# A fused S4 convolution and gated MLP on one core: the order of all operations written as one explicit list

## The chip, the cores and the metric

The kernel runs on one core of a Trainium2 chip. A core has four compute engines, TensorE (PE), VectorE (DVE), ScalarE (ACT) and GpSimd (POOL), and a fifth, SyncE (SP), which issues transfers; each takes its instructions strictly in the order in which the program gives them to it, and waits at the head of its queue until what an instruction needs is there. The metric is device time in microseconds (us), the median over several runs. The profile's span is the time from the first to the last recorded event of one execution; the device time is a little longer.

## The reference

With x = u of shape (1, 2048, 640), the output is a gated sum of two branches:

```python
g = sigmoid((x * gate_w).sum(-1, keepdims=True))
return g * a + (1 - g) * b
```

Branch a is a state space (S4) layer. For each of the 640 channels it forms a kernel K of length 2048 from 128 complex modes, and convolves u with it by FFTs of length 4096:

```python
P = exp(logdA[:, :, None] * l[None, None, :])      # logdA = dt * A, l = 0..2047
K = einsum('dn,dnl,dn->dl', Cc, P, dB).real
y = irfft(rfft(pad(u)) * rfft(pad(K)))[:L] + u * Dskip
```

Branch b is a gated MLP with a product over positions:

```python
z = gelu(x @ w_in)                     # (2048, 1728)
z1, z2 = z[..., :864], layernorm(z[..., 864:])
b = (z1 * (w_sp @ z2 + b_sp)) @ w_out  # w_sp is (2048, 2048)
```

## The kernel before

**How the work is cut.** The 2048 positions are 16 tiles of 128 rows or 8 blocks of 256. The 640 channels are split in two: h0 (480 channels) and h1 (160). The stages, with the names that the profile shows:

- `z2_tile` (L592, 16 tiles): x by the second half of w_in into the two-bank accumulator `two`, then on ACT a gelu (L596) and a tanh for the gate (L598), and sums for the layer norm on ACT or DVE. `z1_tile` (L624, four x groups of four tiles each): the first half of w_in, gelu on ACT into `zt` (L415), stored to DRAM.
- `sp_block` (eight blocks tb 0 to 7): `w_sp` by z2n (L812, 16 matmuls of 128x256 for each of seven tiles of 128 features, recorded in chunks of four), the sum with b_sp on DVE (L816), the product with z1 on DVE (L818), w_out (L832), and a scaling by 1 - g into `ob` (L836 on DVE or ACT). `ob` goes to DRAM except for the last rows, which stay in `acc`.
- `k_exps`, `k_tables`, `eights`: for eight groups of 80 channels, c 0 to 7, tables of exponentials and sines, on ACT, DVE and POOL. POOL or DVE makes the arguments (`si`, `ci`, through L361), ACT takes the sine (L415); ACT loads a table of its own for each of gelu, exp and sine when it changes over.
- `k_sub` (L1045, L1046, eight in all: six for h0, two for h1): 320 small matmuls that make K from the tables. `k_store` and `k_expand` put K out to DRAM and back in the layout of a transform.
- `s1_u` (L651) and `conv_s1` (L1134): the first stage of the transform, of u (from the tile `xf`) and of K, each stored to DRAM (`FU_d`, `FK_d`).
- `conv_s2` (32 steps k for h0, 16 for h1): second stage of u (mu, L1181, copied to `us` on ACT), second stage of K (mk, L1188, `ps_s2k`), their product `p` on DVE (L1190), the first stage back (mv, L1196), copied to `vs` on ACT (L1198).
- `conv_vt` (L1204): 16 DVE transposes of `vs`, three groups of four for h0 (g 0 to 2) and one for h1 (g 3). `conv_i2` (L1276, L1278): the last stage back, which needs all transposes of its half; `i2_out` adds g times it to the MLP's rows (DVE L1212, or ACT L1229 and an add at L1231 on DVE or POOL). A few matmuls without use (L1282) stand ahead of the first of them. Then the output goes out.

**What sets the order.** Nothing in this code runs when it is called. `Plan.add` records each operation as a task: the engine or engines that may do it with a cost for each, the function that emits it, what it reads and writes, and which buffers of a ring it holds. 1810 tasks are recorded. `Plan.run` then goes through them when the program is built and emits them in the order that it finds, and that order is what each engine's queue has. Before the change, `run` is a list scheduler: it keeps a clock for each engine, and when one is free gives it the ready task with the longest remaining path (`bl`) plus a bias. The biases come from the calls and from a table, `TUNE`, keyed by function, line within the function and index. Where a task has several engines, the one that is free takes it. A cost of 1.3 us is charged where ACT's function set changes, and a task may have a `lag` on another: `k_sub` asks for 4.0 us behind the one before it.

Buffers that bear on the order: two of `two` (two PSUM banks each), two of `g` and two of `x` in PSUM; in SBUF, two of `wT` (the blocks of w_sp) and `z1t`, four of `vT`, two of `ob` and `s1u`, one of `xf`, three of `us`, `fu`, `fk` and `p12`.

Of the kernel before, what the change touches and what calls it, by code (L numbers as in the profile page):

```python
# [25 lines left out]
class Handle:  # L26
# [11 lines left out]
TUNE = {  # L38
    ('conv_s1', 18, None): -5520,
    ('conv_s1', 15, ('g', 0)): -124,  # L40
    ('conv_s1', 19, None): 5553,
    ('conv_s2', 35, None): -5280,
    ('conv_s2', 34, ('h', 0)): 2234,
    ('conv_s2', 34, None): 886,
    ('conv_s2', 10, None): 5448,
    ('conv_s2', 14, None): 3353,
    ('conv_s2', 42, None): 2803,
    ('eights', 6, None): 173,
    ('eights', 13, None): 13956,
    ('i2_out', 15, None): 12,  # L50
    ('k_expand', 28, ('h', 0)): 4849,
    ('k_expand', 28, None): 1375,
    ('k_store', 14, ('h', 1)): 2102,
    ('k_store', 6, ('h', 0)): 8481,
    ('k_sub', 13, ('h', 0)): 2159,
    ('k_tables', 31, ('c', 6)): -12493,
    ('k_tables', 31, None): 8580,
    ('k_tables', 32, ('c', 4)): -777,
    ('k_tables', 32, None): 371,
    ('k_tables', 41, None): 1904,  # L60
    ('k_tables', 30, ('c', 7)): 3564,
    ('k_tables', 29, ('c', 3)): -10091,
    ('k_tables', 29, None): 3002,
    ('k_tables', 6, None): 7128,
    ('k_tables', 18, ('c', 7)): 6367,
    ('k_tables', 17, ('c', 4)): 2780,
    ('k_tables', 17, None): -1891,
    ('k_tables', 36, None): 3593,
    ('k_tables', 20, None): -429,
    ('k_tables', 21, ('c', 2)): -5305,  # L70
    ('k_tables', 21, ('c', 6)): -5859,
    ('k_tables', 38, ('c', 6)): 4382,
    ('k_tables', 38, None): -6392,
    ('main', 151, ('g', 0)): -1177,
    ('main', 151, ('g', 3)): 41101,
    ('main', 155, None): -414,
    ('main', 148, None): -2063,
    ('main', 147, None): -1758,
    ('main', 417, None): -6232,
    ('main', 369, None): 2196,  # L80
    ('main', 437, None): 310,
    ('main', 442, None): -153,
    ('main', 419, None): -10,
    ('main', 421, None): -41,
    ('s1_u', 13, ('h', 1)): -11176,
    ('s1_u', 13, ('n0', 0)): -23393,
    ('s1_u', 13, ('n0', 8)): -7946,
    ('s1_u', 13, None): 3018,
    ('s1_u', 16, ('n0', 10)): -8951,
    ('s1_u', 3, ('n0', 0)): -14093,  # L90
    ('s1_u', 3, ('n0', 10)): 63,
    ('s1_u', 3, None): 84,
    ('s1_u', 18, ('h', 1)): 582,
    ('s1_u', 18, ('n0', 12)): -9089,
    ('s1_u', 14, ('h', 1)): -3707,
    ('s1_u', 14, ('n0', 0)): 7218,
    ('sp_block', 23, ('tb', 6)): 5972,
    ('sp_block', 23, None): -1436,
    ('sp_block', 25, ('tb', 5)): -2260,
    ('sp_block', 20, ('tb', 2)): 14630,  # L100
    ('sp_block', 41, ('tb', 1)): 8742,
    ('sp_block', 41, None): 2551,
    ('sp_block', 47, None): -8196,
    ('sp_block', 3, ('tb', 5)): 4372,
    ('sp_block', 3, ('tb', 7)): -14321,
    ('sp_block', 3, None): -4356,
    ('sp_block', 8, ('tb', 5)): 1880,
    ('sp_block', 6, ('tb', 5)): 321,
    ('tg_build', 22, None): 5697,
    ('tg_build', 6, None): -428,  # L110
    ('tg_build', 20, None): 8012,
    ('tg_build', 9, ('c', 0)): 5213,
    ('tg_build', 9, ('c', 1)): 3260,
    ('x_group', 3, None): -2923,
    ('z1_tile', 17, None): 3575,
    ('z1_tile', 10, ('g', 0)): 774,
    ('z1_tile', 10, ('g', 2)): 1445,
    ('z2_tile', 12, None): 5932,
    ('z2_tile', 19, None): 12871,
    ('z2_tile', 18, ('h', 0)): 6796,  # L120
}
HELPERS = ("dma", "actf", "evac", "<lambda>", "ptt", "pts", "ftt", "fts", "pstt", "S_", "E", "K_", "M_")


class Plan:

    ENG = ("PE", "DVE", "ACT", "POOL", "SP", "NONE")
    SYNC = 0.04  # L130
    OV = {"DVE": 0.08, "ACT": 0.09}
    LAT = {"PE": 0.17, "POOL": 0.8}
# [10 lines left out]
    def add(self, eng, cost, fn, r=(), w=(), hold_=(), fset=None, nbytes=0, hold=0.0, bias=0.0, deps=(), lag=()):  # L143
        f = sys._getframe(1)
        while f.f_code.co_name in HELPERS:
            f = f.f_back
        nm = f.f_code.co_name if len(f.f_code.co_name) < 26 else "main"
        rel = f.f_lineno - f.f_code.co_firstlineno
        ix = next(((v, f.f_locals[v]) for v in ("tb", "c", "g", "h", "n0") if isinstance(f.f_locals.get(v), int)), None)
        bias += TUNE.get((nm, rel, None), 0) + (TUNE.get((nm, rel, ix), 0) if ix else 0)  # L150
# [26 lines left out]
    def run(self):  # L177
        T = self.tasks
        N = len(T)
        succ = [[] for _ in T]  # L180
        for t in T:
            for d in t["deps"]:
                succ[d].append(t["i"])
        bl = [0.0] * N
        for t in reversed(T):
            i = t["i"]
            c = min(t["costs"]) + (2.2 + t["nb"] / 1e6 if t["nb"] else 0.0)
            bl[i] = c + max([bl[s] for s in succ[i]], default=0.0)
        users = {}
        seq, cnt = {}, {}  # L190
        for t in T:
            for h in t["hs"]:
                if h not in users:
                    seq[h] = cnt.get(h.ring, 0)
                    cnt[h.ring] = seq[h] + 1
                users.setdefault(h, [0, 0.0])[0] += 1
        nd = [len(t["deps"]) for t in T]
        rdy = [0.0] * N
        allocs = {k: 0 for k in self.rings}
        freed = {k: [] for k in self.rings}  # L200
        slot = {}
        ready = {e: [] for e in self.ENG}
        free = {e: 0.0 for e in self.ENG}
        dma = 0.0
        cold = 0.0
        fset = None
        done = [False] * N
        order = []
        for t in T:
            if nd[t["i"]] == 0:  # L210
                for e in t["engs"]:
                    ready[e].append(t["i"])
        ev = [0.0]
        while len(order) < N:
            if not ev:
                held = {h.ring: [] for h in slot}
                for t in T:
                    if not done[t["i"]] and any(h in slot for h in t["hs"]) and nd[t["i"]] == 0:
                        print("HELD", t["i"], t["engs"], t["fn"].__qualname__[-20:], t["fn"].__code__.co_firstlineno, [(h.ring, h in slot) for h in t["hs"]])
                raise AssertionError("stuck")  # L220
            now = heapq.heappop(ev)
            while ev and ev[0] <= now + 1e-9:
                heapq.heappop(ev)
            again = True
            while again:
                again = False
                for e in self.ENG:
                    if free[e] > now + 1e-9 and e != "NONE":
                        continue
                    best, bk = None, None  # L230
                    for i in ready[e]:
                        if done[i] or rdy[i] > now + 1e-9:
                            continue
                        t = T[i]
                        ok = True
                        for h in t["hs"]:
                            if h in slot:
                                continue
                            a = allocs[h.ring]
                            n = self.rings[h.ring]  # L240
                            if h.ring not in self.free_order and seq[h] != a:
                                ok = False
                            if a >= n:
                                f = freed[h.ring]
                                if a - n >= len(f) or f[a - n] is None or f[a - n] > now + 1e-9:
                                    ok = False
                        if not ok:
                            continue
                        key = bl[i] + t["bias"]
                        if e == "ACT" and t["fset"] and t["fset"] != fset:  # L250
                            key -= 25.0
                        if bk is None or key > bk:
                            best, bk = i, key
                    if best is None:
                        continue
                    again = True
                    t = T[best]
                    i = best
                    done[i] = True
                    for x in t["engs"]:  # L260
                        ready[x] = [j for j in ready[x] if j != i]
                    c = t["costs"][t["engs"].index(e)]
# [3 lines left out]
                    for h in t["hs"]:  # L266
                        if h in slot:
                            continue
# [1106 lines left out]
```

## Time and profile before

| | us |
|---|---|
| device time, median of 3 runs | 357.02 |
| the runs | 356.61, 357.02, 362.8 |
| span of the profiled execution | 353.6 |
| PE busy (L812 alone) | 309.6 (106.8) |
| DVE busy (L1190 alone) | 286.4 (48.4) |
| ACT busy | 241.8 |
| POOL busy | 153.6 |
| first `k_sub` starts | 105.0 |
| first mk of `conv_s2` h0 starts | 263.0 |
| last p of h0 ends | 303.2 |
| first matmul of `conv_i2` starts | 318.8 |

An engine's busy time is a sum over stages which have different limits, so it says little by itself. The page has a table of the span in 40 slices (each 8.8 us), where each digit is an engine's busy share in tenths, and the trace answers the same for any stretch. The list of waits has, for an engine and a line, what it last waited for: total us, times, longest. The chain is followed back from the last instruction, at each step to what released it. The letters PEld stand for TensorE's weight loads, which run beside its matmuls. PEclk is the clock that TensorE was granted, in shares of full speed.

The table by stages, in words: up to 105 us z2, z1, the first blocks and the first tables; from 105 to 248 the six k_subs of h0 and two of h1 among sp_blocks and `s1_u`, with PE busy for 0.88 to 0.97 of the time; 248 to 264 the last blocks; from 264 `conv_s2` of h0; from 305 to 319 its transposes; then `conv_i2` of h0 mixed with `conv_s2` of h1; from 338 the rest of h1, and the output.

### The profile page before, as it was taken

Reading aid. Unit: us, or ns where it says so; the run is one execution under the profiler, and the core shown is the slowest. Engines: PE = TensorE matmul, PEld = TensorE weight load, DVE = VectorE, ACT = ScalarE, POOL = GpSimd, SP = SyncE. Lnnn points to the kernel's source line nnn. Section 1 sums busy time; section 2 is a strip of 40 time slices with the busy share of each in tenths; the row PEclk is TensorE's granted clock in tenths of the full one; section 3 lists DMA queues with packets and bytes.
Section 4 is the critical chain, followed back from the end, with each engine's and each line's share of the span. In section 5 each row is a group of like instructions: output and inputs, shape, how many; then the busy total and the mean of one; then the engine's idle time right before and its main releaser. Section 6 shows DMA issues by size and latency. Waiting matters only on the chain.

```text
span 353.6 us, 8393 instructions
## 1 busy us (share of the span) xinstructions
PE 309.6 (88%) x3231; PEld 216.9 (61%) x3237; DVE 286.4 (81%) x548; ACT 241.8 (68%) x437; POOL 153.6 (43%) x155
## 2 busy tenths in 40 slices
PE   3899899989899999999699998699999999809982
PEld 3455445857778687878577776477774444405751
DVE  4079996789897949998489758777789999996985
ACT  1658975999784676889876684564538888804842
POOL 3005544600095826773187989434459400203221
PEclk9999999999999999999899999899999999977998
DMA  7988999669981578496592249998958886273404
GB/s 200 205 141 230 199 188 213 193 154 191 249 135 49 135 173 164 114 223 104 152 250 82 61 63 174 197 264 267 230 161 250 222 238 195 61 211 138 141 28 130
DMA packets 110809, 59.89 MB, mean 169 GB/s; under 512 B 78322, under 2 KB 107354, under 8 KB 110770
## 3 DMA queue, kind: packets, MB, share of 16 engines
q1 hardware_dynamic: 108530, 55.33, 63.9%
q0 software_dynamic: 2240, 4.04, 5.4%
q8 instruction: 25, 0.41, 0.5%
q14 instruction: 14, 0.11, 0.1%
HBM read 25.25 MB, written 19.47 MB: 126 GB/s over the span
## 4 chain that ended last, share of the span: by engine, by line
PE 44%; DVE 24%; ACT 10%; issue 7%; DMA 6%; POOL 5%; SPq 2%; ACTq 0%; DVEq 0%; POOLq 0%
PE ps_g L812 13%; DVE p L1190 5%; DVE vs L1204 5%; PE ps_z L592 5%; PE ps_o L832 4%; PE ps_z L624 4%; DMA xf<-in_A_u_dram 4%; PE ps_s2k L1188 3%; POOL ci L361 3%; PE ps_k L1045 3%; PE ps_v L1196 3%; PE ps_k L1046 3%; PE ps_s1k L1134 2%; ACT z2n L596 2%; ACT ET L415 2%
## 5 line engine op out<-in xcount | busy, mean ns | idle before, releaser
L812 PE MATMUL ps_g<-wT,z2n 128*128 128x256 bf16 (+1 forms) x896 | 106.8, 276 | 5.8 <-issue 2.8
L812 PEld LDWEIGHTS <-z2n 128*128 128x128 bf16 (+1 forms) x896 | 90.2, 103 | 22.7 <-issue 8.7
L1190 DVE TENSOR_TENSOR p<-ps_s2k,us 128x960 bf16<-128x960 f32 (+1 forms) x48 | 48.4, 1040 | 1.9 <-PE ps_s2k L1188 0.6
L361 POOL TENSOR_SCALAR ci<-ai 128x640 int32<-128x640 int32 (+1 forms) x8 | 21.5, 2693 | 55.3 <-DVE ai L968 33.2
L361 POOL TENSOR_SCALAR si<-th 128x80 int32<-128x80 f32 x40 | 32.1, 802 | 12.7 <-DVE t3p L761 4.6
L832 PE MATMUL ps_o<-Wout,vT 128*128 128x320 bf16 (+1 forms) x224 | 34.3, 299 | 3.0 <-ACT ob L836 3.0
L624 PE MATMUL ps_z<-xg,Win 128*128 128x512 bf16 (+1 forms) x134 | 31.6, 380 | 0.8 <-ACT zt L415 0.5
L592 PE MATMUL ps_z<-Win,xT 128*128 128x432 bf16 (+1 forms) x160 | 30.4, 346 | 2.1 <-ACT gl L598 2.1
L415 ACT ACTIVATE ET<-ci 128x640 bf16<-128x640 int16 (+1 forms) x40 | 26.0, 677 | 6.9 <-POOL ci L361 3.5
L832 PEld LDWEIGHTS <-vT 128*128 128x128 bf16 (+1 forms) x224 | 21.8, 98 | 13.5 <-issue 4.1
L1045 PE MATMUL ps_k<-ET 128*32 128x33 bf16 x640 | 27.7, 259 | 1.6 <-DVE ET L1028 1.1
L1045 PEld LDWEIGHTS <-ET 128*32 128x32 bf16 x640 | 26.9, 193 | 3.6 <-DVE ET L1028 3.1
L1198 ACT CAST vs<-ps_v 128x480 bf16<-128x480 f32 (+1 forms) x48 | 24.3, 521 | 5.1 <-PE ps_v L1196 4.1
L1046 PE MATMUL ps_k<-ET 128*32 128x33 bf16 x640 | 27.6, 258 | 0.0
L1046 PEld LDWEIGHTS <-ET 128*32 128x32 bf16 x640 | 27.1, 195 | 0.3 <-issue 0.3
L816 DVE TENSOR_TENSOR vT<-ps_g,br 128x512 bf16<-128x512 f32 (+1 forms) x32 | 18.7, 615 | 9.8 <-PE ps_g L812 9.8
L1188 PE MATMUL ps_s2k<-fk,T 128*128 128x480 bf16 (+1 forms) x128 | 25.0, 304 | 1.5 <-DVE p L1190 1.4
L1196 PE MATMUL ps_v<-p,G 128*128 128x480 bf16 (+1 forms) x128 | 25.1, 304 | 0.5 <-DVE p L1190 0.2
L592 PEld LDWEIGHTS <-xT 128*128 128x128 bf16 x160 | 15.5, 98 | 16.3 <-issue 3.0
L415 ACT ACTIVATE mr<-lre 128x320 bf16<-128x320 f32 x66 | 25.1, 457 | 0.0
L422 ACT CAST us<-ps_u 128x480 bf16<-128x480 f32 (+1 forms) x48 | 24.0, 521 | 0.7 <-ACT vs L1198 0.4
L415 ACT ACTIVATE ET<-ai 128x640 bf16<-128x640 int16 (+1 forms) x24 | 15.2, 645 | 12.1 <-DVE ai L968 12.1
(195 smaller groups left out, 618.7 us busy)
## 6 DMA issues: line engine op xcount, KB each, us to landing
FU_d<-s1u SPq DMA_DIRECT2D x16, 240.0 KB, 3.4
fu<-FU_d SPq DMA_DIRECT2D x16, 240.0 KB, 3.9
fk<-FK_d SPq DMA_DIRECT2D x16, 240.0 KB, 3.5
z_d<-zt SPq DMA_DIRECT2D x24, 128.0 KB, 2.5
z1t<-z_d SPq DMA_DIRECT2D x8, 384.0 KB, 4.3
xf<-in_A_u_dram SPq DMA_DIRECT2D x8, 320.0 KB, 3.4
Win<-in_B_w_in_dram SPq DMA_DIRECT2D x2, 1080.0 KB, 6.2
ob_d<-ob SPq DMA_DIRECT2D x12, 160.0 KB, 3.3
```

Of the source, the lines that this page charges most:

```text
L361: eng.tensor_scalar(out=out_, in0=in_, scalar1=s1, scalar2=None, op0=op0)
L415: return add("ACT", cost, lambda e: act.activation(out=out_(), in_=in_(), func=func, scale=scale), r=r, w=w, fset=fs, bias=bias, deps=deps ...
L592: pe.matmul(ps()[:, h, 0:432 + h], lhsT=xT[:, i, 128 * st:128 * st + 128], rhs=Win2[:, i, 432 * h:432 * h + 432 + h], start=(i == 0), stop ...
L624: pe.matmul(ps()[0:fs, ft - f0, :], lhsT=Win1[:, i, 128 * ft:128 * ft + fs], rhs=xg()[:, i, :], start=(i == 0), stop=(i == ND - 1))
L812: pe.matmul(ps()[0:fs, ft - f0, :], lhsT=z2n[:, st, 128 * ft:128 * ft + fs], rhs=wT()[:, st, :], start=(st == 0), stop=(st == NS - 1))
L832: pe.matmul(ps()[:], lhsT=vT[ft // 2]()[0:fs, ft % 2, 128 * r:128 * r + 128], rhs=Wout[0:fs, ft, HD * h:HD * h + HD], start=(ft == 0), sto ...
L1045: pe.matmul(o_, lhsT=ET[:, 0:32, d], rhs=M2[:, :, d], start=True, stop=False, tile_position=(0, 32 * q))
L1046: pe.matmul(o_, lhsT=ET[:, NA:NA + 32, d], rhs=E2[:, :, d], start=False, stop=True, tile_position=(0, 32 * q))
L1188: pe.matmul(ps()[:, i, W * n:W * n + W], lhsT=TK(k + n, i), rhs=fk()[:, j + n, :], start=True, stop=True)
L1190: add("DVE", dv1(2 * NW), lambda e, p12=p12, ps=ps, us=us: vec.tensor_tensor(out=p12()[:, :, 0:NW], in0=ps()[:, :, 0:NW], in1=us()[:, 0:NW ...
L1196: pe.matmul(pv()[:, W * n:W * n + W], lhsT=GV(k + n, i), rhs=p12()[:, i, W * n:W * n + W], start=(i == 0), stop=(i == 1))
L1198: add("ACT", 0.15 + NW / 1170, lambda e, k=k, pv=pv: act.copy(out=X["vs"][h][:, k:k + NK, :], in_=pv()[:, 0:NW].rearrange("p (k d) -> p k ...
```

## The change

`run` no longer schedules. A text, `ORDER`, has three characters for each of the 1810 tasks: two for its number, one for its engine (0 PE, 1 DVE, 2 ACT, 3 POOL, 4 SP). `run` reads it, asserts that every task is there once, that its engine is one of those allowed and that its dependencies come first, takes buffers and emits. `TUNE` and the scheduler's model are gone. The order and the engines in the list were found by a search that moves single tasks, with durations from a trace. The tasks, their functions, the pools and the rings are the same. Some costs in the calls are changed too, but nothing reads them now. Two small things besides: POOL is no longer among the engines of the copy into M2 (L993), and a `k_sub` has a plain dependency on the one before it.

```diff
-TUNE = {
-    ('conv_s1', 18, None): -5520,
...
-}
+A64 = "ABCDEFGHIJKLMNOPQRSTUVWXYZabcdefghijklmnopqrstuvwxyz0123456789+/"
+ORDER = """
+AS2AY1AX1AV1AW1Dz1AU3Ad0Ae0AT1Af0Ag0AD4DQ5Ah0AC4AA4Dy1D11D01D20Aa0Ac2AB4Ai0Ao0AZ2Ap2AQ3AJ4Aj0AH4Ab0AI4Ak0AE4AK4D31Aq2Ar1AG4DR1Au0DU1Al1AF4C+4A40Av2Cq4
...
+be4cO1cQ1bj4cM4cR4bv1bw2bx1by4
+"""
...
     def run(self):
         T = self.tasks
...
-                    c = t["costs"][t["engs"].index(e)]
-                    if e == "ACT" and t["fset"] and t["fset"] != fset:
-                        c += 1.3
-                        fset = t["fset"]
...
+        text = "".join(ORDER.split())
+        num = lambda k: A64.index(text[k]) * 64 + A64.index(text[k + 1])
+        order = [(num(k), int(text[k + 2])) for k in range(0, len(text), 3)]
+        assert sorted(i for i, _ in order) == list(range(len(T)))
+        done = set()
...
+        for i, e in order:
+            t = T[i]
+            assert self.ENG[e] in t["engs"] and t["deps"] <= done
+            done.add(i)
+            for h in t["res"]:
                 h()
-            T[i]["fn"](e)
-            for h in T[i]["hs"]:
+            t["fn"](self.ENG[e])
+            for h in t["hs"]:
                 left[h] -= 1
                 if left[h] == 0:
                     h.t = None
...
-        add(("DVE", "ACT", "POOL"), (0.2, 0.27, 0.6), lambda e: act.copy(out=M2()[:, 0:1, :], in_=mr(0, 1)) if e == "ACT" else E_[e].tensor_copy(out=M2()[:, 0:1, :], in_=mr(0, 1)), r=[("mr", 0, zm)],
+        add(("DVE", "ACT"), (0.2, 0.27), lambda e: act.copy(out=M2()[:, 0:1, :], in_=mr(0, 1)) if e == "ACT" else E_[e].tensor_copy(out=M2()[:, 0:1, :], in_=mr(0, 1)), r=[("mr", 0, zm)],
...
-        tab_ids.append(add("PE", 3.65, m, r=tabs + (["cva"] if h else []), w=[ps], bias=8000, lag=[(tab_ids[-1], 4.0)] if tab_ids else []))
+        tab_ids.append(add("PE", 3.35, m, r=tabs + (["cva"] if h else []), w=[ps], bias=8000, deps=tab_ids[-1:]))
```

What the list does to the queues, engine by engine, from the two programs' instruction orders: the z1 tiles of the second x group come in one run; the first k_sub has less of the sp_blocks ahead of it; `conv_s2` of h0 begins before sp_blocks 6 and 7 are done, and their matmuls and those of `conv_s1` of h1 stand between its steps; the transposes of h0 alternate with the products of h1; all of `conv_i2` comes last, that of h1 first. Engines change for single operations, as the table has them.

| operation | moves |
|---|---|
| `si` | POOL to DVE 5, DVE to POOL 3 |
| `ci` (from si) | DVE to POOL 6, POOL to DVE 4 |
| `ci` (from ai) | POOL to DVE 6, DVE to POOL 5 |
| copy into M2 (L993) | POOL to DVE 1, ACT to DVE 1, DVE to ACT 3 |
| add of `i2_out` (L1231) | POOL to DVE 6, DVE to POOL 2 |
| scaling into `ob` or `acc` (L836) | DVE to ACT 12, ACT to DVE 2 |
| copy of `conv_s1` | DVE to ACT 7, ACT to DVE 4 |
| copies of `s1_u` | ACT to DVE 7, DVE to ACT 6 |
| transfers of `k_store`, `k_expand`, `conv_s1` | POOL to SP 23, SP to POOL 17 |

## The prediction

> **What bounds the kernel now.** I read the page's busy table first, then the slices, then the chain that ended last.
>
> ```profile
> PE 309.6 (88%) x3231; PEld 216.9 (61%) x3237; DVE 286.4 (81%) x548; ACT 241.8 (68%) x437; POOL 153.6 (43%) x155
> ...
> PE   3899899989899999999699998699999999809982
> ...
> DVE  4079996789897949998489758777789999996985
> ...
> PEclk9999999999999999999899999899999999977998
> ...
> PE 44%; DVE 24%; ACT 10%; issue 7%; DMA 6%; POOL 5%; SPq 2%; ACTq 0%; DVEq 0%; POOLq 0%
> ```
>
> TensorE is the bound on average, but the end is not one TensorE queue: the chain is only 44% PE. The 0 and 7s near the end of the PE and PEclk rows are one hole. The table by stretches (columns: stretch, its length, then busy us of PE, PEld, DVE, ACT, POOL, clock, DMA share, GB/s) shows it between stages of different limits:
>
> ```profile
> 50.00:105.00 55.00, 50.85 (x393) 38.45 (x391) 46.54 (x103) 46.99 (x78) 17.77 (x19) 1.00 0.85 192
> 105.00:154.00 49.00, 47.72 (x759) 37.80 (x760) 42.05 (x86) 32.70 (x53) 31.47 (x24) 1.00 0.59 137
> ...
> 264.00:303.00 39.00, 37.50 (x185) 17.05 (x183) 38.23 (x43) 33.05 (x65) 13.14 (x18) 1.00 0.75 214
> 303.00:319.00 16.00, 5.17 (x33) 2.98 (x32) 15.54 (x15) 5.36 (x10) 1.82 (x2) 0.82 0.58 158
> 319.00:338.00 19.00, 18.46 (x173) 13.39 (x172) 16.03 (x21) 13.58 (x33) 5.46 (x5) 0.88 0.35 114
> ```
>
> 264 to 303 us is conv_s2 of h0, with DVE full: 32 products p (L1190) of 1.15 us pitch. From 303 to 319 DVE alone works. The chain names what it does there, and the list of waits who stands still:
>
> ```profile
> 304.92 13.84 DVE vs L1204 x12
> 318.81 1.76 PE ps_i L1278 x4
> ```
>
> ```profile
> PE ps_i L1278 <- DVE vs L1204: 9.3, 1, 9.3
> ```
>
> Twelve transposes in one block keep PE idle for 9.3 us. Earlier, the first k_sub (L1045) starts at 105.0; until then ACT builds its tables, from the first exp at 63.7 to the last sine's end at 102.9.
>
> **What the change does to the order.** No operation is removed or added: 1810 tasks, the same buffers. I laid the traced durations of before along both orders: "work ahead" is the sum of traced durations queued before an instruction on its engine. Total PE work is 300.9 us in both. A few operations change engine, and with the durations of their new engine DVE goes from 280.6 to about 282.5, ACT from 224.9 to 226.1 beside 14.1 us of table loads, POOL from 147.5 to about 120. The one visible saving inside that is the POOL copy of 8.40 us (L993, ET<-mr), which becomes 0.2 us on DVE or ACT; POOL is not the bound, so I cost it at nothing by itself.
>
> *Step 1, up to the first k_sub.* Before, the second x group's z1 tiles (L624) are interleaved with sp_block 0; after, they come in one run: the last of them has 47.9 us of PE work ahead of it, not 50.9, and the third z2 tile no longer waits 1.26 us for two gelus (L596, 0.89 each) to be done, since ACT now gives gelu and tanh in tile order. The first exp follows the last z1 gelu: 63.7 before, and 3.0 + 1.3 + about 1.4 of the waits between those z1 tiles earlier, so 58. From there ACT has 28.6 us of work to the last sine of table 0 (30.3 before, where 5.1 of table loads and 3.8 of waits made it 39.2): 58 + 28.6 + 5.1 = 91.7, then the last product of the table on DVE, 1.9, and 1.4 of waits: **95** for k_sub 0. Bounds: 93.6 without a wait, 105.0 if ACT still waits as before. DVE (75.2 us of work ahead, begun 12 to 14 late: 89) and PE (76.8 ahead, 83 with the idle start) would allow it. I take 95 since ACT's waits in that stretch were DVE's (ai L968 3.0 of 3.8), and DVE's work ahead falls too, 75.7 to 73.3.
>
> *Step 2, from k_sub 0 to the last mk (L1188, k31) of conv_s2 h0.* PE work ahead of k_sub 0 is 76.8 (90.6 before); of mk k31 270.1 (268.9). So 193.3 us of PE work lie between, and PE is the limit: DVE's stretch is 240.4 - 75.2 = 165.2. The new order starts conv_s2 when 210.7 us of PE work are done (233.4 before) and weaves sp_blocks 6 and 7 and conv_s1 of h1 between its 32 steps. In before 35.5 us of PE work met 36.1 of DVE work from mk k0 to k31; now 59.4 meet 46.4: the DVE-bound stage becomes PE-bound. What it costs beyond the work is PE's lost time L. Before lost 17.6 us between these two points (26.2 lost up to k31, 8.6 up to k_sub 0). Of it 7.5 are four stops at places of the old order: xf's load 2.67 (at 169), an issue 2.85 (at 224), 1.19 (at 216), 0.81 (at 136). 2.6 belong to the DVE-bound stretch. The remaining 7.5 are many waits under 0.8 us. The first two sorts have their places moved; I let them go and keep the small ones: **L = 7.5**. Bounds: 0 (the list fits exactly), and 17.6 (each stop comes back elsewhere). Nothing excludes more; the rival below prices it.
>
> *Step 3, the end.* p k31 ends 1.6 us after mk k31 starts. The transposes (1.29 each) are not one block now: the first stands between h1's products and most of them alternate with those (0.82 each), so DVE goes on working and conv_s2 of h1 fills PE; all of conv_i2 (L1276, L1278) comes last, with the last Wout group and the warming matmuls (L1282) ahead of it. After p k31 DVE has 282.5 - 241.5 = 41.0 us of work. I add 1.5 for waits (before it waited 3.1 there: 2.3 for PE, 0.8 for ACT) and 3.5 from the last compute (350.0) to the end of the span: **46.0**, against 353.6 - 303.2 = 50.4 before. So the 9.3 us of PE idle are worth only 4.4: DVE is what is late next. POOL-to-DVE adds of i2_out (net four, 0.3 to 0.4 on DVE) are inside the 41.0.
>
> What hides the rest: SP has 177 us of issue work before and 181 after, 30 more issues taken from POOL; they cost nothing while SP's queue is idle half the span. If that cover goes, a load behind a store that waits for its data is late by a transfer, 3.4 us for xf, 4.3 for z1t.
>
> **Sum.** 95 + 193.3 + 7.5 + 1.6 + 46.0 = 343.4 us of span. The profiled span of before is 353.6 and the median of its runs 357.02, so 3.4 lie around it: **346.8**, that is 2.9% faster. About 2% is what a measurement of this kernel can tell from no change.
>
> **The clock.** After the hole the granted clock is 0.50 from 318.0 to 320.5, 0.74 to 326 and 1.00 from there; four matmuls of conv_i2 took 1.76 us at its start and 0.82 later. [...] In this trace the price of one such spell is about 1 us for each four matmuls in the first 5.5 us, some 3 to 6 us in all; my 1.5 of waits has no room for it, and the range does.
>
> **Rivals.**
> *The stalls only move.* An order fitted to one execution's durations loses as much at run time as the old one: L = 17.6, span 353.5, time 356.9. For it: in-order queues wait for the latest of several engines, and POOL's ci<-ai, beside DVE's work, took 1.00 to 5.16 us, so no list knows them. Against it: steps 1 and 3 come from work that leaves the chain, not from fitted waits; but with k_sub 0 at 100 and L = 12 the time is 356 also.
> *The list fits.* L between 0 and 4 with step 1 and 3 as worked out: span 336 to 340, time 339 to 343. For it: PE's largest stops are all tied to the old order's places.
> *Slower.* One mechanism: the weave in conv_s2. Each g tile of sp_blocks 6 and 7 (eight; two buffers) must be read by a DVE add (L816, 0.62) that now stands in DVE's queue behind a product of 1.15, which itself waits for an mk queued on PE behind the sp matmuls. If each of the 32 steps loses one such round, 1.15 less the 0.3 to 0.5 hidden, it is 0.7 x 32 = 22 us on L's 7.5: span 365.8, time 369. It decides from L = 25 on (time over 364.2), about half of the steps.
>
> **Chances.** Forecast (342 to 350): 0.47. The list fits: 0.18. Stalls move (350 to 364): 0.24. Slower: 0.11. Faster by over 2% (under 349.9) is 0.65, within it 0.24, slower 0.11. The range takes L from 0 to 17.6 and leaves out the slower case and a sliver of the others: 338 to 359.
>
> **What would show it.** Step 1: the first k_sub at 93 to 97 us, the first exp at 58. Step 2: mk k31 near 296 (95 + 193.3 + 7.5), PE at 9s from slice to slice in conv_s2, DVE no longer at 98% there. Step 3: no block of transposes in the chain, no PE gap over 3 us after p k31, 46 us from there to the end. I am wrong if k_sub 0 starts later than 100, if PE loses over 12 us in step 2, or if conv_i2 runs at a clock of 0.5 to 0.75.

## The result and the profile after

The changed kernel took 345.85 us in the median (345.36 to 347.17, four runs), the kernel before 356.81 (with a fourth run, 355.52, beside the three known): a ratio of 0.9683, 95% interval 0.9638 to 0.9729, so 3.2% faster. The profiled execution took 347.17 us with a span of 345.4.

The page of the changed kernel, busy time, two rows of the slices, the clock and the shares of the chain:

```profile
PE 306.7 (89%) x3237; PEld 215.8 (62%) x3237; DVE 290.0 (84%) x560; ACT 242.7 (70%) x438; POOL 126.0 (36%) x141
...
PE   3899998698789999999799989999999999966871
...
DVE  4169999989999999989894889666965699999984
...
PEclk9999999989989999999899999999999999999997
...
PE 45%; DVE 25%; ACT 8%; DMA 7%; issue 5%; SPq 5%; POOL 2%; ACTq 0%; DVEq 0%; POOLq 0%
```

The hole near the end of the PE and PEclk rows is gone: between the first slice and the last none has a PE share under 6 tenths, and the clock is below 8 tenths only in the last slice. DVE has its thin slices earlier now (8 8 9 6 6 6 9 6 5 6), where PE is full, and full ones at the end. The table by stretches, in the columns of the first one, shows the same for the places that the prediction spoke of:

```profile
264.00:303.00 39.00, 37.90 (x247) 22.67 (x245) 32.73 (x37) 30.50 (x60) 2.72 (x3) 1.00 0.72 211
303.00:319.00 16.00, 10.32 (x126) 8.90 (x127) 16.00 (x19) 8.95 (x25) 0.00 (x0) 1.00 0.44 125
319.00:338.00 19.00, 15.09 (x98) 9.30 (x96) 17.72 (x27) 7.84 (x17) 3.84 (x7) 1.00 0.19 57
```

From 303 to 319 DVE is busy all the time, as before, but PE does 10.32 us of work beside it where it did 5.17. The chain still names DVE's transposes (L1027 here) as one block of eight, the last ones, but in the list of waits PE waits 1.4 us for a transpose, not 9.3:

```profile
318.28 1.08 DVE vs L1027
...
319.39 9.33 DVE vs L1027 x8
328.72 1.70 DVE wT L1035 x5
```

```profile
PE ps_s2k L1011 <- DVE p L1013: 2.9, 5, 0.9
...
PE ps_i L1101 <- DVE vs L1027: 1.4, 1, 1.4
```

The dates of the two traces, and the lengths between them:

| | before, us | after, us |
|---|---|---|
| last z1 gelu ends | 62.4 | 58.5 |
| first exp starts | 63.7 | 59.8 |
| last sine of table 0 ends | 102.9 | 93.4 |
| k_sub 0 starts | 105.0 | 97.0 |
| mk k0 of h0 starts | 263.0 | 238.8 |
| mk k31 of h0 starts | 301.1 | 296.3 |
| p k31 of h0 ends | 303.2 | 298.3 |
| end of the span | 353.6 | 345.4 |

So of the 8.2 us of span, 4.9 are won up to p k31 and 3.3 behind it. (k_sub 0 is 8.0 earlier, but 3.1 of that is gone again at p k31.) The trace of before is of one of its shorter executions and that of the changed kernel of the longest of its four, so the two show 8.2 of the 11.0 us between the medians.

### The profile page after: what moved, and what is told of

It reads as the page before. It is cut to its first block, busy times and chain, and to the rows that moved or that the text cites. A ratio compares the mean times of both kernels' runs of the same rounds, so it can differ in the third digit from the quotient of the medians.

```text
span 345.4 us, 8358 instructions
## 1 busy us (share of the span) xinstructions
PE 306.7 (89%) x3237; PEld 215.8 (62%) x3237; DVE 290.0 (84%) x560; ACT 242.7 (70%) x438; POOL 126.0 (36%) x141
## 4 chain that ended last, share of the span: by engine, by line
PE 45%; DVE 25%; ACT 8%; DMA 7%; issue 5%; SPq 5%; POOL 2%; ACTq 0%; DVEq 0%; POOLq 0%
PE ps_g L635 12%; PE ps_z L415 8%; PE ps_z L447 6%; DVE vs L1027 5%; DVE p L1013 4%; PE ps_o L655 4%; ACT ET L238 3%; PE ps_s2k L1011 3%; PE ps_v L1019 3%; SPq L233 3%; PE ps_s1k L957 2%; DVE s1u L245 2%; PE ps_k L868 2%; POOL ci L184 2%; PE ps_k L869 2%
## 5 line engine op out<-in xcount | busy, mean ns | idle before, releaser
L635 PE MATMUL ps_g<-wT,z2n 128*128 128x256 bf16 (+1 forms) x896 | 109.9, 274 | 2.7 <-DVE vT L639 1.6
L184 POOL TENSOR_SCALAR si<-th 128x80 int32<-128x80 f32 x48 | 35.3, 735 | 16.5 <-DVE ai L791 4.7
L1021 ACT CAST vs<-ps_v 128x480 bf16<-128x480 f32 (+1 forms) x48 | 24.6, 520 | 12.8 <-PE ps_v L1019 12.3
L447 PE MATMUL ps_z<-xg,Win 128*128 128x512 bf16 (+1 forms) x140 | 33.0, 391 | 0.0
L415 PE MATMUL ps_z<-Win,xT 128*128 128x432 bf16 (+1 forms) x160 | 31.8, 359 | 0.0
L238 ACT ACTIVATE ET<-ci 128x640 bf16<-128x640 int16 (+1 forms) x40 | 26.8, 680 | 6.1 <-POOL ci L184 3.5
L639 DVE TENSOR_TENSOR vT<-ps_g,br 128x512 bf16<-128x512 f32 (+1 forms) x32 | 19.7, 617 | 12.3 <-PE ps_g L635 11.7
L184 POOL TENSOR_SCALAR ci<-ai 128x640 int32<-128x640 int32 (+1 forms) x6 | 15.9, 2652 | 38.6 <-ACT ET L238 27.0
L238 ACT ACTIVATE zt<-ps_z 128x1024 bf16<-128x1024 f32 (+1 forms) x16 | 14.5, 914 | 14.9 <-PE ps_z L447 7.3
```

The source lines that it names most:

```text
L184: eng.tensor_scalar(out=out_, in0=in_, scalar1=s1, scalar2=None, op0=op0)
L238: return add("ACT", cost, lambda e: act.activation(out=out_(), in_=in_(), func=func, scale=scale), r=r, w=w, fset=fs, bias=bias, deps=deps ...
L415: pe.matmul(ps()[:, h, 0:432 + h], lhsT=xT[:, i, 128 * st:128 * st + 128], rhs=Win2[:, i, 432 * h:432 * h + 432 + h], start=(i == 0), stop ...
L447: pe.matmul(ps()[0:fs, ft - f0, :], lhsT=Win1[:, i, 128 * ft:128 * ft + fs], rhs=xg()[:, i, :], start=(i == 0), stop=(i == ND - 1))
L635: pe.matmul(ps()[0:fs, ft - f0, :], lhsT=z2n[:, st, 128 * ft:128 * ft + fs], rhs=wT()[:, st, :], start=(st == 0), stop=(st == NS - 1))
```

## The experiments

All of them are the changed kernel with another list, so the operations and buffers are the same; their line numbers are one less than those of the changed kernel (L1012 is p, L1026 the transposes). Beside the experiments the kernel before took 357.5 to 359.0 us, 1 to 2 us more than beside the changed kernel, so ratios are compared.

| run | median us | ratio to before | 95% interval |
|---|---|---|---|
| the changed kernel | 345.85 | 0.968 | 0.964 to 0.973 |
| 1 old order as a list | 357.25 | 0.997 | 0.993 to 1.002 |
| 2 new head, old rest | 382.72 | 1.069 | 1.061 to 1.078 |
| 3 old head, new rest | 370.25 | 1.032 | 1.023 to 1.042 |
| 4 old tail | 353.83 | 0.987 | 0.980 to 0.994 |
| 5 k_sub 0 later | 349.86 | 0.975 | 0.968 to 0.982 |
| 6 new order, old engines | 375.07 | 1.046 | 1.040 to 1.052 |
| 7 no weave | 355.45 | 0.991 | 0.988 to 0.995 |
| 8 transposes in a block | 354.55 | 0.989 | 0.982 to 0.996 |
| 9 old order, new tail | 368.51 | 1.027 | 1.021 to 1.033 |
| 10 old order, new engines | 377.05 | 1.052 | 1.046 to 1.058 |
| 11 three waits mended | 345.97 | 0.966 | 0.962 to 0.970 |
| 12 no weave and block | 363.04 | 1.018 | 1.010 to 1.027 |

### 1. The old order as a list

```diff
-ORDER = the new list
+ORDER = the order and engines of the kernel before
-add(("DVE", "ACT"), (0.2, 0.27), ...            # copy into M2
+add(("DVE", "ACT", "POOL"), (0.2, 0.27, 0.6), ...
```

> The order and engines of the kernel before, written as the list of the changed kernel (POOL again allowed for the copy into M2). If only order and engines matter: the time of the kernel before, 356 to 358. If the list itself, the plain dependency of k_sub or another part of the diff carries the gain: under 352.

Ratio 0.997, no difference. Order and engines are all of the change.

### 2, 3 and 4. One part new, the rest old

The new order is cut at the start of k_sub 0 (runs 2 and 3) or at the product p of step 31 (run 4); what the first part had not done follows in the order of the other kernel, and a task that isn't ready or finds no buffer is taken as soon as it can be.

```diff
 run 2: new order up to k_sub 0
-       new order from there
+       old order from there
```

> The new order up to the start of the first k_sub, the old order for all that is left. Theory of the prediction's step 1 (k_sub 0 eight us earlier is a gain by itself): 356.8 - 8 = 349. Rival (PE's account: the new head has 13.8 us less PE work done when k_sub 0 starts, so the work is only owed): 97.0 + 224.1 us of PE work left + the 32.1 that the old order lost after k_sub 0 + 6.1 from the last matmul to the end + 1.8 around the span = 361, no gain.

```diff
-run 3: new order up to k_sub 0
+       old order up to k_sub 0
        new order from there
```

> The old order up to the start of the first k_sub, the new order for all that is left. Theory of step 1: its gain is gone, 345.9 + 8 = 354. Rival (PE's account): 105.0 + 210.3 us of PE work left + 17.4 that the new order lost after k_sub 0 + 5.8 to the end + 1.8 = 340, faster than both kernels; somewhere between, 343 to 348, if the later tables then stop PE.

```diff
 run 4: new order up to p of step 31 of h0
-       new order from there
+       old order from there
```

> The new order up to the product p of step 31 of h0, then the old order: twelve transposes in one block, conv_i2 of h0 mixed with conv_s2 of h1. Theory of step 3 (the tail is DVE's work, so the hole in PE costs little): the tails were 50.4 and 47.1 us, so 345.9 + 3.3 = 349. Rival (the 9.3 us of idle PE and the clock behind it are the loss): 354 to 356.

Runs 2 and 3 took 382.7 and 370.3 us, far outside of both theories. The longest waits of PE, of run 2, of run 3 and of run 4 in turn, tell a part of why:

```profile
PE ps_o L654 <- ACT s1u L244: 12.5, 2, 10.9
```

```profile
PE ps_s1x L477 <- ACT ob L658: 11.0, 2, 9.2
```

```profile
PE ps_i L1100 <- DVE vs L1026: 13.0, 1, 13.0
```

In run 2 the new head had issued an s1_u matmul whose copy stands in ACT's queue at its old place, behind sines that are not due yet; it starts at 141.9 us. Until then its PSUM buffer is held, and PE's next Wout group waits 10.9 us for it. In run 3 the same happens with a scaling into `ob` on ACT (L658), for which an s1_u matmul waits 9.2 us. So the seams cost 9 to 11 us at one place each; the rest of what the two runs lost was not traced. They say nothing on the worth of an early k_sub 0; run 5 does.

Run 4 has a seam too. Its tail is 54.0 us (p k31 ends at 298.2, the span at 352.2), against 47.1, with the hole back. That looks like 7 us for the hole instead of the 3.3 expected, and it led to run 8. But DVE's queue in run 4, where the last number in brackets is the idle time ahead, shows that a part lies ahead of the block:

```profile
300.88 0.55 DVE L183 TENSOR_SCALAR acc<-ps_o,omg 128x320 bf16<-128x320 f32 x1 [2.70 <-PE ps_o L654]
301.83 0.55 DVE L183 TENSOR_SCALAR acc<-ps_o,omg 128x320 bf16<-128x320 f32 x1 [0.40 <-PE ps_o L654]
303.63 13.79 DVE L1026 STREAM_TRANSPOSE vs<-vs 128x640 f32<-128x640 f32 x12 [1.25 <-ACT vs L1020]
```

DVE stands idle for 4.35 us between p k31 and its first transpose, where the kernel before has 0.22: that is the seam. From the first transpose to the end it is 48.6 us in run 4 and 48.7 in the kernel before. Less the seam, the tail of run 4 is about 50 us (an estimate from these numbers), as the old one was, and the expected 3.3 us stand. The run doesn't show that the hole costs 7.

### 5. k_sub 0 later

```diff
 TensorE's queue
-  k_sub h0 s0
   z1_tile g2 f00, f02; sp_block 1: f4 c0 to c12, f6 c0, f5 c0, f6 c4; z1_tile g2 f04
+  k_sub h0 s0
```

> The new order with one task and its copy moved: k_sub 0 stands behind the next ten TensorE tasks (9.5 us of PE work) instead of ahead of them. Theory of step 1 (an earlier k_sub 0 is a gain by itself): 345.9 + 9.5 = 355. Rival (PE's account: what counts is that PE has work; the tables have slack): 346, up to 349 if the work put ahead isn't ready at 97 us.

k_sub 0 started at 110.0 us instead of 97.0, and the span grew by 3.4 (348.8): the rival. k_sub 1 was 3.1 us later, and mk k31 2.7 (299.0). Of 13 us of delay, about ten were slack. The intervals of the two ratios, 0.968 to 0.982 and 0.964 to 0.973, overlap, so even these 3.4 us aren't clear of noise.

### 6 and 10. Order and engines exchanged

```diff
 run 6: ORDER = the new order of tasks
-       the new engine of each task
+       its old engine
```

> The new order of tasks, but each on the engine that it had before: POOL has 26.8 us more work, DVE 2.7 less, ACT 1.2 less. If the order alone is the gain: 343 to 347 (DVE's 2.7 us less in the tail's favour). Rival (order and engines belong together: a task on a slower engine is late in a queue that was made for the faster one): over 352.

```diff
 run 10: ORDER = the old order of tasks
-        the old engine of each task
+        its new engine
```

> The order of before with the engines of the changed kernel. If the engine changes are a gain by themselves (POOL's work falls by 26.8 us, its 8.4 us copy is gone): 350 to 356. If order and engines belong together, as the sixth run says: 365 or more.

136 of the 1810 tasks have another engine in the two lists. By the lists and the traces, three rows of the table of moves are a little different: scaling into `ob` or `acc` DVE to ACT 7, ACT to DVE 5; copy of `conv_s1` DVE to ACT 8, ACT to DVE 3; copies of `s1_u` ACT to DVE 8, DVE to ACT 5.

Both runs are slower than the kernel before, 375.1 and 377.1 us. In run 6 the loss grows all along: k_sub 0 at 104.8, mk k0 at 260.8, p k31's end at 321.1, and a tail of 52.0. No single wait carries it; from PE's list of waits of run 6:

```profile
PE ps_o L654 <- ACT s1u L244: 5.6, 2, 4.9
PE ps_o L654 <- DVE ob L183: 4.2, 3, 2.5
PE ps_g L634 <- DVE vT L638: 3.7, 4, 2.4
```

and from that of all its engines, where ACT's sines wait for POOL:

```profile
ACT ET L237 <- POOL ci L183: 9.7, 6, 3.1
```

The engine choices are no gain by themselves, and the order none without them. The waits fit one reading: a task that comes to a queue which was not made for it waits there behind others, or makes them wait. The tasks were not tried one by one.

### 7. No weave

```diff
 TensorE, DVE and ACT
-  conv_s2 h0 k0 to k21 between the tasks of sp_blocks 6 and 7
   sp_blocks 6 and 7 up to the last matmul of w_sp
+  conv_s2 h0 k0 to k21
   conv_s2 h0 from there on
```

> The new order, but conv_s2 of h0 starts only when the last matmul of w_sp of sp_block 7 is issued: from mk k0 to mk k31 32.5 us of PE work then meet 33.3 of DVE work (32 products of 1.15 us pitch: 37), where it was 59.4 and 47.9. Theory of step 2: the stage is DVE's again, PE loses 4 to 6 us more, 350 to 352. Rival (the weave is not needed, the earlier tables are): 346 to 347.

Ratio 0.991: the weave is worth 2.3%, 8 us. mk k31 starts at 303.7 instead of 296.3, and the tail is as long as with the weave, 47.3 us (305.7 to 353.0). The stretch from mk k0 to mk k31, in this run and in the changed kernel:

```profile
264.20:303.70 39.50, 34.41 (x154) 14.32 (x153) 34.08 (x33) 30.30 (x60) 0.00 (x0) 1.00 0.71 209
```

```profile
238.80:296.30 57.50, 56.78 (x367) 35.65 (x366) 46.71 (x64) 38.42 (x71) 14.79 (x20) 1.00 0.72 200
```

PE loses 5.1 us there without the weave and 0.7 with it. That is 4.4 of the 7.4 us; the other 3 lie ahead of the stretch and have no single name. (conv_s1 of h1 is done ahead of conv_s2 in this run, at 256 to 262 us.) DVE and PE each work for about 34 of 39.5 us, and both wait; PE's waits for p in mk and mv grew only from 2.9 + 2.6 us to 4.0 + 3.5, but the mean pitch of a step from mk k0 to k31 is 39.5 / 31 = 1.27 us, where DVE's product needs 1.15 and PE's part 1.07 (0.26 + 0.40 + 0.41, the traced pitches of mu, mk and mv). Neither engine reaches its own limit; DVE also waits 2.7 us for the copies into `us` on ACT. Taken by the ratio, 0.991 x 356.8 = 353.7, the expected 350 to 352 was about 2 us too low.

### 8. The transposes in a block

```diff
 DVE's queue
   p h1 k0, k2
+  eleven of the twelve transposes of h0 (the first stands there already)
-  p h1 k4 to k30, with seven of the transposes between them
+  p h1 k4 to k30
   the transposes of g3
-  the other four of h0
```

> The new order with the twelve transposes of h0 in one block, ahead of the third product of h1, as the kernel before had them. Theory of step 3 (the tail is DVE's work, 41 us in either order): PE stands still 9 to 10 us longer there and the end moves by 0 to 2: 346 to 348. Rival (the block's hole in PE and the clock behind it cost what the old tail cost in the fourth run, 7 us): 352 to 354.

Ratio 0.989, 2.1% for moving DVE work within DVE's queue: the rival, by its number; its ground, the 7 us of run 4, doesn't stand. The tail is 55.8 us (295.8 to 351.6) against 47.1. The stretches of run 8:

```profile
297.00:304.00 7.00, 2.25 (x24) 1.68 (x22) 6.99 (x7) 2.23 (x6) 0.00 (x0) 0.95 0.34 107
304.00:311.00 7.00, 0.00 (x0) 0.00 (x0) 7.00 (x8) 0.00 (x0) 0.00 (x0) 0.50 0.00 0
311.00:318.00 7.00, 6.19 (x52) 6.00 (x52) 4.77 (x7) 3.30 (x9) 0.00 (x0) 0.57 0.34 88
318.00:327.00 9.00, 7.17 (x90) 6.16 (x88) 6.22 (x8) 6.40 (x18) 0.00 (x0) 1.00 0.53 152
```

and those of the changed kernel for the same work:

```profile
298.30:319.40 21.10, 14.85 (x173) 12.47 (x173) 21.09 (x25) 12.43 (x33) 0.00 (x0) 1.00 0.51 142
319.40:328.70 9.30, 7.54 (x60) 5.66 (x58) 9.30 (x10) 2.83 (x7) 1.86 (x4) 1.00 0.00 0
```

DVE's work in the tail is nearly the same, 41.7 us and 41.0 in the changed kernel, but its idle time grows from 6.1 us to 14.1. In the changed kernel the transposes lie where DVE would wait: while PE and ACT prepare the next product, DVE has a transpose to do. In run 8 the block comes first, and then DVE waits between the products: it is busy 4.77 of 7.00 us while PE is at a clock of 0.57, and 6.22 of 9.00 when the clock is full again. Of the 8 us more, only 1.8 (0.78 and 1.04, waits between products) fall into the half-clock stretch, so most of it is not the clock. Two waits have names in the list of run 8:

```profile
DVE p L1012 <- ACT us L244: 4.0, 5, 1.0
DVE wT L1034 <- PE ps_u L1098: 2.2, 1, 2.2
```

The second is the wait for the first matmuls of conv_i2; in the changed kernel these start at 324.1, beneath the last transposes of h0.

But the block isn't dear in every order. In run 4 it stands too, and there nine products of h1 run back to back:

```profile
329.02 7.69 DVE L1012 TENSOR_TENSOR p<-ps_s2k,us 128x640 bf16<-128x640 f32 x9
```

So PE and ACT can prepare them at DVE's pace. In that order, as in the kernel before, conv_i2 of h0 stands between the products of h1 ahead of them. From the first transpose to the end it is 48.6 us in run 4 and 54.3 in run 8, which has two products less to do there. The block costs 8 us in an order that was made for spread transposes and has conv_i2 last; which part of PE's or ACT's order makes DVE wait there was not tried.

### 9. The old order with the new tail

```diff
 old order up to p of step 31 of h0
-old order from there
+new order from there
```

> The old order up to the product p of step 31 of h0, the new order for the rest: transposes between the products of h1, conv_i2 last. If the tail's length belongs to the tail alone: 303.2 + 47.1 + 1.8 = 352 to 353, 4 us faster than before. If the block of transposes is worth in the old order what it was worth in the new one (7 to 8 us): 349 to 350. If the tail needs what the new middle has prepared (conv_s1 of h1 is not done yet at that point): 356 or more.

The third case, and more: 368.5 us. From the list of waits of run 9:

```profile
PE ps_s2k L1010 <- DMA fk<-FK_d: 9.1, 1, 9.1
```

In this run conv_s1 of h1 is done from 305.4 to 310.6 us (302.6 to 307.8 in the kernel before); its output goes to DRAM and back before the first mk of h1, and that takes PE 9.1 us of waiting. In the kernel before, the block of transposes lay over this transfer, from 304.9 to 318.8 us. SP issues it there at these times:

```profile
307.37 1.58 SPq L410 DMA_DIRECT2D FK_d<-s1k  x2
314.78 1.76 SPq L410 DMA_DIRECT2D fk<-FK_d  x4
```

The loads land 3.8 us behind their issue (median), so the first mk of h1 could hardly start before 318 (an estimate): the hole in PE had two causes, and the block was not the only one. In the changed kernel conv_s1 of h1 is done from 266 to 280, within the weave, and the first mk of h1 starts 0.8 us behind mk k31's end.

### 11. Three waits mended

```diff
 TensorE's queue
+  sp_block 0: f3 c0, c4, c8, c12
   s1_u n02 ab0
-  sp_block 0: f3 c0, c4, c8, c12
 ...
-  s1_u n014 ab0, second matmul
   sp_block 4: f1 c4; k_sub h0 s4
+  s1_u n014 ab0, second matmul
 SP's queue
   wT of sp_block 1, first half
+  xf of n02
   five other transfers
-  xf of n02
```

> The new order with three places mended where PE stood still: four matmul chunks of sp_block 0 ahead of the s1_u that waits 2.9 us for xf at 66 us, that xf load 1.4 us earlier in SP's queue, and one matmul of s1_u that waits 1.8 us at 167 put behind k_sub 4. If PE's waits count wherever they are: 2.9 + 0.9 less, 342. If ACT and DVE bound the stretch from 57 to 97 us (97% and 94% busy there), the first two give nothing and the third 0.9: 345.

345.97 us, ratio 0.966: no difference from the changed kernel that can be told, so the version isn't better. PE's wait for xf (2.9 us) is gone, and k_sub 0 starts at 97.1 as before. The third wait is gone too, and in its place k_sub 4 waits 1.3 us for a scaling into `ob` on ACT. The waits of PE between 57 and 97 us in run 11, and the stretch:

```profile
PE ps_g L634 <- DVE vT L638: 4.2, 3, 2.2
PE ps_o L654 <- ACT s1u L244: 2.4, 1, 2.4
```

```profile
57.00:97.00 40.00, 31.00 (x233) 23.41 (x231) 37.88 (x77) 38.68 (x66) 22.94 (x22) 0.94 0.81 193
```

PE now waits for DVE and ACT instead, which are 95% and 97% busy. They bound this stretch, and what PE loses in it is no reserve.

### 12. Both edits of runs 7 and 8

```diff
 TensorE, DVE and ACT
-  the weave
+  conv_s2 h0 behind sp_block 7, as in run 7
 DVE's queue
-  the transposes between the products of h1
+  the transposes in a block, as in run 8
```

> The new order with both edits of the seventh and eighth run: conv_s2 of h0 only behind the last w_sp matmul of sp_block 7, and the twelve transposes of h0 in one block. If the two costs are independent (ratios to the kernel before of 0.991 and 0.989 where the new order has 0.968: 2.3% and 2.1%): ratio 1.012, slower than the kernel before. If they are one gain seen twice (a DVE-bound stage and a hole that each hide part of the other): ratio 0.99, as with one of them.

Ratio 1.018 (1.010 to 1.027): the two costs add. p k31 ends at 306.1 us as in run 7, and the tail is 55.5 us as in run 8. Without these two arrangements the new order is slower than the old, by 1.0 to 2.7%.

## Why the prediction was right, and where not

The forecast was 346.8 us with a range of 338 to 359; 345.85 was measured.

**Around the span.** The prediction set the profiled span of before, 353.6, against the median of the runs, 357.02, and put 3.4 us around it. In the changed kernel each run has its span beside its time, and the difference is 1.8 (347.17 and 345.4, 345.56 and 343.8). The profile of before belongs, by the same 1.8, to an execution of about 355.4, a faster one than the median. So the term was 1.6 us too large, and the sum of the span, 343.4, was 2.0 too small for the profiled one. The two errors cancel but for 0.4 us: that the forecast is within 1 us of the median is luck.

**Step 1, k_sub 0 at 95:** it started at 97.0, within the bounds. The first exp came at 59.8, not 58, the 28.6 + 5.1 us of ACT from there came out as 33.6, and the last product ended 3.5 us behind the last sine, not 1.9 + 1.4. The late exp doesn't come from the z1 tiles: PE is busy for 46.77 of the 46.80 us from 10.2 us on. It comes from the start, where PE waits for the load of gate_w and the first x tile then takes 3.65 us for its ten matmuls, not 2.10. The kernel before has the first line, the changed one the others:

```profile
9.82 2.10 PE L592 MATMUL ps_z<-Win,xT 128*128 128x432 bf16 x10
```

```profile
9.37 0.18 PE L375 MATMUL pt_s<-ident,gw 5*128 5x5 bf16 x1 [3.07 <-DMA gw<-in_gate_w_dram]
10.20 3.65 PE L415 MATMUL ps_z<-Win,xT 128*128 128x432 bf16 x10
```

Every run with the new head shows it (a wait of 3.1 to 3.7 us, 3.3 to 3.8 us for the ten matmuls), none with the old. The clock column says 1.00 in both, but in the changed kernel's trace the first record of the clock begins only at 13.6 us, behind nearly all of these ten matmuls (9.3 in that of before, ahead of them), so why they are slower stays open.

But run 5 shows that the date by itself isn't a gain: about ten of 13 us of delay are slack. Nor is PE's lost time in that stretch one (run 11). The term stands in the sum because PE's work is counted from there on; as an explanation of the gain it falls.

**Step 2, 193.3 us of work and 7.5 lost:** mk k31 came 199.3 behind k_sub 0, so 6.0 were lost where 17.6 were before. The mechanism is shown by run 7: without the weave mk k31 comes 7.4 us later with the same PE work ahead, and 4.4 of them are lost between mk k0 and mk k31. The rival that the stalls only move is out. So is its opposite, a list that fits: L was above 4. Which of the old stops would come back was a choice, and that 7.5 was near is luck in part. Of the stops that I let go, the one for xf is not gone: PE waits 2.9 us for it at 66 us, ahead of k_sub 0, where run 11 shows that it costs nothing.

**Between them, 1.6 us** from mk k31's start to p k31's end: it is 2.0. So the parts of the span are 97.0 + 199.3 + 2.0 + 47.1 = 345.4.

**Step 3, 46.0 us of tail:** it is 47.1. The 41.0 us of DVE work are there to a tenth (40.99 in the windows from 298.3 to the end); the waits are 2.5 and the way out is 3.6, where I had 1.5 and 3.5. The step said that the hole in PE is worth only what DVE's work and waits leave, "DVE is what is late next". For the two kernels that it compared this holds: 42.0 us of DVE work and 8.4 of the rest before, 41.0 and 6.1 after; and run 4, less its seam, gives the old tail back. As a rule it doesn't: run 8 gives back the hole alone, with DVE's work nearly unchanged, and it costs 8.7 us of tail, because DVE then waits 8 us more. The old tail was only 50.4 long since its block covered a transfer (run 9) and since conv_i2 of h0 stood between the products of h1, where DVE then had no such waits (run 4 beside run 8).

**The slower rival,** one PE wait for a w_sp tile's add in each of 32 steps, 22 us: PE's waits for that add (L639) are 1.6 us in all, two times, and none of it lies within the weave.

**The clock.** I gave 3 to 6 us of range for a tail at a low clock. The granted clock is 1.00 in the stretches from 298.3 to 341 us; what PE does there is spread, with the L1105 matmuls started between 317.9 and 325.6, and no gap up to its last matmul is over 1.45 us. Run 8 shows the other case: PE stands still for 12.3 us, from 299.5 to 311.8, and the clock is 0.50 from 304 to 311 and 0.57 in the 7 us behind. Shorter gaps are followed by a low clock too: in the changed kernel PE waits 2.90 us up to 68.9 and 1.75 us up to 168.6, and behind them the clock is 0.50 for some 3.3 us:

```profile
68.20:71.50 3.30, 2.57 (x11) 1.57 (x12) 3.30 (x4) 3.30 (x6) 3.11 (x4) 0.50 1.13 231
170.60:173.90 3.30, 3.30 (x108) 2.58 (x105) 3.16 (x10) 3.10 (x8) 1.27 (x2) 0.50 0.87 175
```

The clock is 0.50 from 98.9 to 102.3 as well, where PE's longest wait in the 10 us ahead is 1.33 us, while behind the two of 1.45 us in the tail it is 1.00. So the absence of gaps over 3 us doesn't by itself show a full clock here, and from which length on a gap has a low clock behind it, the runs don't show; the measurement decides. The price of run 8's gap is mostly DVE's waits, as the stretch at full clock shows.

Still open: why the rest of the new order, without the two arrangements, loses 1.8% to the old one. By the dates of run 12 against those of before, 5.1 us are lost in the tail (55.5 against 50.4, the block without the old mix behind it) and 2.9 ahead of it (p k31 ends at 306.1, not 303.2), though conv_s1 of h1 is done by then. Open is also what each of the engine changes is worth; no run moved one of them alone. The 8.4 us POOL copy, which I cost at nothing, was not tried by itself either.

## What to carry to other kernels

Put a stage that one engine bounds beside a stage that another bounds, step by step in the queues: two such pairings (w_sp blocks with conv_s2, transposes with the h1 products) were taken out of the new order at a cost of 2.3% and 2.1%, and both together turn its gain of 3.2% into a loss of 1.8%. Against the kernel before the second is worth less, since that order had another cover for its block. A hole may cover something else, so look what runs beneath it (here a transfer that cost PE 9.1 us when it lay bare) before its length is booked as a gain. An explicit order and its engine choices are one thing: half of a list spliced to half of another, or engines exchanged under it, cost 2.7 to 6.9% against the kernel before (all but run 4), so single changes are to be tried as moves of a few tasks in the whole list.

## What the runs showed that was not expected

- Moving k_sub 0 by 13.0 us cost 3.4 us of span, and by the ratios even that is not clear of noise.
- Moving eleven transposes within one engine's queue, with the same operations on every engine, cost 2.1% in the new order; in the old one the block cost little.
- PE gaps of 2.90 and 1.75 us were followed by some 3.3 us at a granted clock of 0.50.
- The lists with parts or engines of the other order are all slower than the kernel before by 2.7 to 6.9%, but for the one that was cut late and kept the new order up to p k31 (0.987).
